# Clustered attention with a feed-forward block on one core: queries laid out lower half first, one copy less, the keys' copies moved to GpSimd and VectorE, and two prices of the planner changed

## The chip, the core and the metric

The kernel runs on one core of a Trainium2 chip. The core has a matrix engine (TensorE, in the profile PE, with its weight loads as PEld), a vector engine (VectorE, DVE), a scalar engine (ScalarE, ACT), a general engine (GpSimd, POOL) and a queue engine that only starts DMA transfers here (SyncE, SP). Each engine carries out its own list of instructions in order; semaphores make one wait for another. The time is device microseconds of the core, from one launch; lower is better.

## The reference

Two parts follow each other. Attention has 4 batches, 8 heads, 768 positions and 64 dimensions per head. Each query and each key is assigned to one of 16 clusters of its head, and a query sees only keys of its own cluster. The output, 3072 tokens of 512 features, goes through a feed-forward block of 2048 hidden units with a clipped square as its activation.

```python
def _attn_ref(q, k, v, centroids):
    ...
    q_assign = np.argmax(np.einsum('bhsd,hcd->bhsc', q_n, c_n), axis=-1)
    k_assign = np.argmax(np.einsum('bhsd,hcd->bhsc', k_n, c_n), axis=-1)
    mask = q_assign[:, :, :, None] == k_assign[:, :, None, :]
    scores = scale * np.matmul(q, k.transpose(0, 1, 3, 2))
    scores = np.where(mask, scores, -1000000000.0)
    scores = scores - np.max(scores, axis=-1, keepdims=True)
    attn = np.exp(scores)
    attn = attn / (np.sum(attn, axis=-1, keepdims=True) + 1e-09)
    return np.matmul(attn, v).astype(np.float32)

def _moe_ref(x, w_in, w_out):
    h = x @ w_in
    g = np.where(h >= 1, h, np.where(h <= -1, 0.0, (h + 1) ** 2 / 4))
    return (g @ w_out).astype(np.float32)
```

(The second function is shortened: its constant beta is 1.) Everything is float32 in and out.

## The kernel before, in words

**Numbers in two halves.** Every float32 operand of a product is scaled by a power of two and split into an upper and a lower float16 half, and a product is formed as upper times lower plus lower times upper plus upper times upper. So most products come in threes.

**Staging.** The work goes by batch (4), by pair of heads (4 per batch, 16 in all, called head pairs) and by chunk of 256 queries (3). For a head pair, `kv_load` loads keys, queries and values, `kv_scale` finds the scales, `kq_split` makes the halves and `assign` finds the clusters. A score group (`at_scores`) is for 128 queries of one head; there are 192. `at_soft` forms the exponentials on ScalarE, splits them, and transposes them by DMA into the tile `pT` (11 of them early on by TensorE, in groups of six float32 transposes). `at_av` multiplies with the values into `banka`, where each product uses 64 columns of the array. `ffn1` and `ffn2` are the feed-forward block for 256 tokens and 256 hidden units. Its weights are loaded and split in the opening only (`w_load`, `w_bits`, `w_sum`, `w_split`; tiles `w` and `wk`).

**Keys and queries of a head pair.** `kn` and `qn` are tiles of 128 partitions x 12 blocks x 2 x 64 in float16 (in the profile `n`, in the first batch also `x`, `o` and `g`): for each of the 12 blocks (2 heads x 6 tiles of positions) two halves of 64. `kq_split` fills the keys as (lower, upper) and the queries as (upper, lower), and a DMA transpose turns each into `kT` and `qT` (in the tile `kvq`), so that one product over 128 rows gives both mixed terms. `assign` multiplies `kT` and `qT` with the centroids and finds the nearest cluster on VectorE. Then it reuses the same tiles: the first half of each block becomes a code of the cluster (16 columns, written by VectorE; the other 48 of the keys are cleared by GpSimd), the second half must hold the upper halves, for the keys times `phi`, a factor of the head pair. For the keys that is a GpSimd product in place (lines 640 to 642). For the queries, whose second half still holds the lower halves, ScalarE makes a second copy of the upper ones from the float32 queries (lines 645 and 646). Two more DMA transposes give `k1` and `q1`, which carry the third term and the mask. `kT` too is multiplied by `phi` in place, by ScalarE (lines 643 and 644), before the score products read it. The rest of `assign` works out `er`, which the score evictions use.

**Order of the work.** Nothing is issued directly. A recorder collects all operations with their dependences, and `Recorder.issue` plans them: up to eight rounds of a list schedule (`forward`), with due times worked out backwards (`backward`), and the best plan's order is issued engine by engine. What an operation is thought to take comes from `Recorder.price` (line 76): it sees engine, operation and sizes. For TensorE the price is by columns, with a separate rule, `half`, for products with at most 64 columns of weights, and before 75 us of planned time TensorE's prices are doubled. So a change of a price or of one operation can move instructions in the whole program. Since everything is issued from one line, all instructions in the profile have line 292; groups are told apart by their tiles.

Of the kernel before, what the change touches and what calls it, by code (L numbers as in the profile page):

```python
# [11 lines left out]
F32 = mybir.dt.float32  # L12
U32 = mybir.dt.uint32
AF = mybir.ActivationFunctionType
ALU = mybir.AluOpType
# [22 lines left out]
class Recorder:  # L38
# [37 lines left out]
    def price(self, eng, op, out, ins, kw):  # L76

        if "dma" in op:
            n = 1
            for k in out.shape:  # L80
                n *= k
            kb = n * mybir.dt.size(out.dtype) / 1024

            return 33, 79.0 if kb == 2 else kb, "transpose" in op
        n = max(self.free(a) for a in [out] + ins[:1])
        ps = any(a.space == PSUM for a in ins)
        cols = sum(isinstance(kw.get(k), bass.AP) for k in ("scale", "bias", "scalar", "scalar1", "scalar2"))
        if eng == "tensor":
            n = self.free(ins[1])
            half = self.free(ins[0]) <= 64 and n > 100  # L90
            if op == "transpose":
                n *= 2
            elif ins[1].dtype == F32:
                n *= 4
            return n / 4.8 + 1.2 if half else max(n / 2.4 + 2.5, 24)
        if eng == "scalar":
            cols += kw.get("accum_out") is not None
            first = n == 1 and kw.get("scale") == 0.0
            return 93 + n / 1.2 + 94 * cols - 43 * ps + 1283 * first
        if eng == "vector":  # L100
            wide = [a for a in ins if self.free(a) > 1 or n == 1]
            wait = 400 if not ps and (len(wide) > 1 or op in ("tensor_scalar", "tensor_copy")) else 0
            fast = 1
            if op in ("tensor_scalar", "tensor_copy") and not ps:
                fast = 4 if mybir.dt.size(out.dtype) == 2 and mybir.dt.size(ins[0].dtype) == 2 and n > 64 else 2
            return 68 + n / 0.96 / fast + 61 * cols + 20 * (op == "reciprocal") + wait
        return 55 + n * (2.03 if op == "tensor_tensor" else 0.9 if op == "memset" else 3.5)
# [243 lines left out]
def tile_clustered_attention_moe(  # L351
# [11 lines left out]
    B, H, S, D = q.shape  # L363
    C = cent.shape[1]
# [4 lines left out]
    P = 128  # L369
# [21 lines left out]
    rec = Recorder(tc)  # L391
# [37 lines left out]
    def early():  # L429

        return rec.step < EARLY

    def misc(*shape):
        return (row_banks if early() else hid)(*shape, dtype=F32)
# [144 lines left out]
    def transpose(out, nat):  # L579
        rec.sync.dma_start_transpose(out=out, in_=nat.rearrange("p n a d -> p (n a d)"))  # L580

    def kq_split(b, hp):

        e = KV[b, hp]
        for x, lower, at in (("k", 0, 0), ("q", 1, 4)):
            nat = e[x + "n"]
            src = e[x].rearrange("p j (t d) -> p (j t) d", d=D)
            col = "kq".index(x)
            split(nat[:, :, 1 - lower], nat[:, :, lower], src, e["sc"][:, col : col + 1])
            e[x + "T"] = view(e["parts"][at], [2 * T, P], F16)  # L590
            transpose(e[x + "T"], nat)
# [6 lines left out]
    def assign(b, hp):  # L598

        e = KV[b, hp]  # L600
        n2 = 2 * T
        n4 = 2 * n2
        z1 = misc(n4, C)
        for i, x in enumerate("kq"):
            with rec.group():
                for n in range(n2):
                    h = 2 * hp + n // T
                    for a in range(2):
                        rec.tensor.matmul(
                            z1[:, i * n2 + n],  # L610
                            e[x + "T"][:, n],
                            cT[:, a, h * C : (h + 1) * C],
                            start=(a == 0),
                            stop=(a == 1),
                        )
# [9 lines left out]
        rec.vector.tensor_reduce(out=mx, in_=z1, op=ALU.max, axis=AX.X)  # L625
        rec.vector.tensor_tensor(out=z1, in0=z1, in1=wide(mx), op=ALU.subtract)

        rec.gpsimd.memset(e["kn"][:, :, 0, C:], 0.0)
        for i, x in enumerate("kq"):
            rec.vector.tensor_scalar(  # L630
                out=e[x + "n"][:, :, 0, :C],
                in0=z1[:, i * n2 : (i + 1) * n2],
                scalar1=0.0,
                scalar2=-ONE if x == "k" else ONE,
                op0=ALU.not_equal if x == "k" else ALU.is_equal,
                op1=ALU.mult,
            )

        kn, qn = e["kn"], e["qn"]
        rec.gpsimd.tensor_tensor(  # L640
            out=kn[:, :, 1], in0=kn[:, :, 1], in1=e["phi"].unsqueeze(2).to_broadcast([P, n2, D]), op=ALU.mult
        )
        kf = e["kT"].rearrange("p n q -> p (n q)")
        rec.scalar.activation(out=kf, in_=kf, func=AF.Copy, scale=e["phi"])
        qf = e["q"].rearrange("p j (t d) -> p (j t) d", d=D)
        rec.scalar.activation(out=qn[:, :, 1], in_=qf, func=AF.Copy, scale=e["sc"][:, 1:2])
        for x, part in (("k", 3), ("q", 2)):
            e[x + "1"] = view(e["parts"][part], [n2, P], F16)
            transpose(e[x + "1"], e[x + "n"])

        pn = misc(2, C)
        with rec.group():
# [457 lines left out]
```

## Time and profile before

| what | value |
|---|---|
| median of 3 runs | 921.69 us (919.97 to 922.86) |
| the profiled execution's own time | 923.2 us |
| its span, first to last instruction | 921.4 us |
| mean granted TensorE clock | 0.981 |
| TensorE busy | 812.9 us, 88% |
| ScalarE busy | 691.6 us, 75% |
| VectorE busy | 604.1 us, 66% |
| GpSimd busy | 565.6 us, 61% |
| share of the DMA engines taken by transfers | 77.0% |

The span in 40 slices of 23 us each, as tenths of a slice:

```profile
PE   0256668988998999999989999998998999999998
DVE  5998777887888565646776665547886555554222
ACT  6989997977778677778868778777887677777232
POOL 1766786975565577765555667655656677666221
DMA  9979956796899958978999778888899768576100
```

A 9 means 90% or more of the slice. TensorE fills up over the first eight slices, while the other engines are full from the second on. The shares of the whole span are averages over parts with different limits, so the prediction reads them by stretch.

### The profile page before, as it was taken

The numbers are of one execution on the slowest core, as the hardware profiler recorded it, in microseconds if no ns is written. First come the engines' busy times: TensorE is split into PE (matmuls) and PEld (weight loads), VectorE is DVE, ScalarE is ACT, GpSimd is POOL, SyncE is SP. The second block draws the span as 40 slices with busy tenths as digits, with TensorE's granted clock in tenths as the row PEclk, the third lists the DMA queues.
The fourth block names the chain that finished last, engine by engine and source line by source line (L and its number), as shares of the span: only waits on it lengthen the run. The fifth ranks groups of instructions, "written<-read, shape, count | busy, mean of one in ns | idle before, by whom it ended". The sixth has DMA issues, their size and how long they took to land.

```text
span 921.4 us, 19471 instructions
## 1 busy us (share of the span) xinstructions
PE 812.9 (88%) x7414; PEld 559.2 (61%) x7414; DVE 604.1 (66%) x1322; ACT 691.6 (75%) x1173; POOL 565.6 (61%) x520
## 2 busy tenths in 40 slices
PE   0256668988998999999989999998998999999998
PEld 0234446655766766676666666766666666666664
DVE  5998777887888565646776665547886555554222
ACT  6989997977778677778868778777887677777232
POOL 1766786975565577765555667655656677666221
PEclk9998789999999999999999999999999999999999
DMA  9979956796899958978999778888899768576100
GB/s 293 251 176 218 238 127 145 155 188 139 200 179 159 189 109 144 181 130 193 196 186 163 147 150 166 149 175 170 184 179 174 136 136 129 108 130 113 19 24 24
DMA packets 409535, 144.39 MB, mean 157 GB/s; under 512 B 386272, under 2 KB 401632, under 8 KB 409440
## 3 DMA queue, kind: packets, MB, share of 16 engines
q1 hardware_dynamic: 409440, 143.14, 77.0%
q8 instruction: 58, 0.95, 0.4%
q14 instruction: 37, 0.30, 0.1%
HBM read 40.40 MB, written 6.29 MB: 51 GB/s over the span
## 4 chain that ended last, share of the span: by engine, by line
PE 65%; DVE 10%; ACT 6%; issue 5%; POOL 3%; ACTq 0%; DVEq 0%; POOLq 0%
PE bank L292 47%; PE banka L292 10%; PE bankh L292 8%; DVE sS L292 3%; DVE r L292 2%; ACT sS L292 2%; DVE bank L292 2%; POOL hl L292 1%; ACT w L292 1%; DVE bankh L292 1%; DVE mx L292 1%; ACT hl L292 1%; POOL g L292 1%; ACT r L292 1%; DVE n L292 0%
## 5 line engine op out<-in xcount | busy, mean ns | idle before, releaser
L292 POOL TENSOR_TENSOR hl<-sS,hl 128x768 f16<-128x768 f32 x181 | 303.9, 1683 | 148.7 <-ACT hl L292 115.9
L292 PE MATMUL bank<-w,g 128*128 128x512 f16 x1152 | 271.1, 379 | 0.3 <-POOL g L292 0.2
L292 PEld LDWEIGHTS <-w 128*128 128x128 f16 x2304 | 224.4, 98 | 66.8 <-issue 23.0
L292 DVE CUSTOM_DVE_ANT_0 sS<-bank,zero,er 128x768 f32<-128x768 f32 x192 | 194.3, 1012 | 97.7 <-PE bank L292 67.8
L292 PEld LDWEIGHTS <-kvq 128*64 128x64 f16 (+1 forms) x3264 | 191.1, 106 | 86.2 <-issue 41.3
L292 ACT ACTIVATE sS<-sS,sbi 128x768 f32<-128x768 f32 x192 | 179.2, 933 | 83.9 <-DVE sbi L292 80.2
L292 POOL TENSOR_TENSOR g<-r,g 128x512 f16<-128x512 f32 x96 | 112.6, 1173 | 122.8 <-ACT g L292 119.2
L292 PEld LDWEIGHTS <-g 128*128 128x128 f16 x1152 | 110.7, 98 | 119.1 <-issue 2.1
L292 PE MATMUL bank<-kvq 128*128 128x384 f16 x768 | 162.4, 336 | 19.3 <-DVE sbi L292 14.1
L292 ACT CAST hl<-sS 128x768 f16<-128x768 f32 x181 | 148.3, 825 | 4.9 <-DMA pT<-hl 3.7
L292 PE MATMUL bank<-x,w 128*128 128x256 f16 x1032 | 123.9, 272 | 10.5 <-DVE r L292 5.2
L292 ACT ACTIVATE r<-r,f_ra,f_rs 128x512 f32<-128x512 f32 x96 | 77.8, 810 | 70.7 <-DVE r L292 69.7
L292 PE MATMUL banka<-pT,kvq 128*64 128x256 f16 x1728 | 106.4, 279 | 0.0
L292 DVE TENSOR_SCALAR r<-bank,f_lo,f_hi 128x512 f32<-128x512 f32 x64 | 51.6, 807 | 51.0 <-PE bank L292 41.9
L292 POOL TENSOR_TENSOR w<-w 128x1024 f32<-128x1024 f32 (+1 forms) x28 | 59.8, 2143 | 33.9 <-ACT w L292 32.0
L292 ACT CAST g<-r 128x512 f16<-128x512 f32 x96 | 58.8, 612 | 25.2 <-DVE r L292 18.7
L292 DVE SCALAR_TENSOR_TENSOR r<-bank,f_gs,r 128x512 f32<-128x512 f32 x64 | 47.9, 749 | 24.3 <-ACT r L292 15.6
L292 PE MATMUL bank<-wk,w 128*128 128x256 f16 x504 | 61.1, 272 | 3.1 <-DVE bank L292 2.1
L292 PE MATMUL bankh<-x,w 128*128 128x256 f16 x504 | 60.1, 273 | 2.2 <-DVE r L292 2.0
L292 PEld LDWEIGHTS <-ones 128*128 128x128 bf16 x244 | 17.2, 107 | 53.5 <-issue 38.5
L292 DVE TENSOR_SCALAR r<-bankh,f_lo,f_hi 128x512 f32<-128x512 f32 x32 | 25.8, 806 | 25.4 <-PE bankh L292 19.8
L292 ACT ACTIVATE n<-kvq,sc 128x768 f16<-128x768 f32 x42 | 37.1, 924 | 1.7 <-DVE sc L292 1.6
(158 smaller groups left out, 842.5 us busy)
## 6 DMA issues: line engine op xcount, KB each, us to landing
w<-in_moe_w_in_dram SPq DMA_DIRECT2D x14, 512.0 KB, 4.8
w<-in_moe_w_out_dram SPq DMA_DIRECT2D x14, 512.0 KB, 4.7
kvq<-in_k_dram SPq DMA_DIRECT2D x16, 384.0 KB, 3.6
kvq<-in_q_dram SPq DMA_DIRECT2D x16, 384.0 KB, 3.8
kvq<-in_v_dram SPq DMA_DIRECT2D x16, 384.0 KB, 4.1
out_dram<-o SPq DMA_DIRECT2D x11, 512.0 KB, 3.0
o<-in_v_dram SPq DMA_DIRECT2D x8, 384.0 KB, 3.7
pT<-hl SPq DMA_TRANSPOSE x181, 4.0
```

Of the source, the lines that this page charges most:

```text
L292: fn(*args, **kw)
```

## The change

Three things are done.

1. The order of the halves is turned around: keys (upper, lower), queries (lower, upper). The product over 128 rows gives the same two mixed terms. For the queries, the second half now holds the upper halves from the start, and ScalarE's second copy of them is left out, once per head pair.
2. For the keys the second half now holds the lower halves, so GpSimd's product with `phi` reads the first half and writes the second. It is recorded at the beginning of `assign`, ahead of the clearing and of the cluster code, which overwrite the first half. The scaling of `kT` by `phi` goes from ScalarE (`activation`) to VectorE (`tensor_scalar`), recorded behind the two transposes.
3. In `Recorder.price` a transpose is no longer counted twice, but as any float32 operand is, four times (its second operand is the float32 identity), and the fixed part of the `half` products goes from 1.2 to 9 ns.

```diff
-            if op == "transpose":
-                n *= 2
-            elif ins[1].dtype == F32:
+            if ins[1].dtype == F32:
                 n *= 4
-            return n / 4.8 + 1.2 if half else max(n / 2.4 + 2.5, 24)
+
+            return n / 4.8 + 9 if half else max(n / 2.4 + 2.5, 24)
...
-        for x, lower, at in (("k", 0, 0), ("q", 1, 4)):
+        for x, lower, at in (("k", 1, 0), ("q", 0, 4)):
...
         z1 = misc(n4, C)
+
+        kn = e["kn"]
+        rec.gpsimd.tensor_tensor(
+            out=kn[:, :, 1], in0=kn[:, :, 0], in1=e["phi"].unsqueeze(2).to_broadcast([P, n2, D]), op=ALU.mult
+        )
...
-        kn, qn = e["kn"], e["qn"]
-        rec.gpsimd.tensor_tensor(
-            out=kn[:, :, 1], in0=kn[:, :, 1], in1=e["phi"].unsqueeze(2).to_broadcast([P, n2, D]), op=ALU.mult
-        )
-        kf = e["kT"].rearrange("p n q -> p (n q)")
-        rec.scalar.activation(out=kf, in_=kf, func=AF.Copy, scale=e["phi"])
-        qf = e["q"].rearrange("p j (t d) -> p (j t) d", d=D)
-        rec.scalar.activation(out=qn[:, :, 1], in_=qf, func=AF.Copy, scale=e["sc"][:, 1:2])
         for x, part in (("k", 3), ("q", 2)):
             e[x + "1"] = view(e["parts"][part], [n2, P], F16)
             transpose(e[x + "1"], e[x + "n"])
+        kf = e["kT"].rearrange("p n q -> p (n q)")
+        rec.vector.tensor_scalar(out=kf, in0=kf, scalar1=e["phi"], scalar2=None, op0=ALU.mult)
```

The whole plan comes out in another order; three places matter below. The first is ScalarE's list in the opening, from the weights' passes to the scaling of the second head pair's keys. `n_73` and `x_70` with `sc` are float16 halves of queries, `kvq` with `phi` is `kT` being scaled, `kvq` with `sv` the values' halves, `w` and `wk` the weights. Before:

```order
L292 CAST w_76<-w_76 128x1024
L292 ACTIVATE n_73<-kvq_61,sc_137 128x12x64
L292 ACTIVATE kvq_61<-kvq_61,phi_141 128x1536
L292 ACTIVATE kvq_62<-kvq_62,sv_146 128x768
L292 ACTIVATE w_76<-w_76 128x1024
L292 ACTIVATE x_70<-kvq_63,sc_137 128x12x64
L292 ACTIVATE x_69<-kvq_63,sc_137 128x12x64
L292 ACTIVATE wk_66<-w_76 128x1024
L292 ACTIVATE w_76<-w_76,w_sw_158 128x1024
L292 CAST w_76<-w_76 128x1024
L292 ACTIVATE kvq_62<-kvq_62,phi_142 128x1536
```

Now, down to the first exponential (`sS_83`):

```order
L291 ACTIVATE x_69<-kvq_63,sc_137 128x12x64
L291 ACTIVATE x_70<-kvq_63,sc_137 128x12x64
L291 ACTIVATE wk_66<-w_76 128x1024
L291 ACTIVATE g_71<-kvq_64,sc_138 128x12x64
L291 ACTIVATE w_76<-w_76,w_sw_157 128x1024
L291 CAST w_76<-w_76 128x1024
L291 ACTIVATE w_76<-w_76 128x1024
L291 ACTIVATE o_65<-kvq_64,sc_138 128x12x64
L291 ACTIVATE kvq_63<-kvq_63,sv_146 128x768
L291 ACTIVATE kvq_64<-kvq_64,sv_146 128x768
L291 ACTIVATE sS_83,rs_163<-sS_83,sbi_159 128x768
```

The third copy per head pair (`n_73` alone) and both scalings with `phi` are gone, and the splits of the third and fourth head pair have moved up ahead of the first exponential.

The second place is VectorE's list at the first head pair, from the cluster codes (`n_72`, `n_73`) on. Before:

```order
L292 TENSOR_SCALAR n_73<-bank_79 128x12x16
L292 SCALAR_TENSOR_TENSOR kvq_61<-kvq_61,sv_146 128x768
L292 TENSOR_SCALAR wk_66<-wk_66 128x1024
L292 TENSOR_SCALAR has_150<-bankh 128x32
L292 RECIPROCAL bank_79<-es_140 128x1
L292 TENSOR_SCALAR bank_79<-bank_79 128x2
L292 SCALAR_TENSOR_TENSOR w_76<-w_76,wk_66 128x1024
L292 TENSOR_TENSOR bank_79<-bank_79,has_150 128x192
L292 TENSOR_REDUCE bank_78<-bank_78 128x1
```

Now:

```order
L291 TENSOR_SCALAR n_73<-bank_79 128x12x16
L291 RECIPROCAL sc_137<-bank_79 128x2
L291 TENSOR_SCALAR bank_79<-bank_79 128x1
L291 TENSOR_SCALAR wk_66<-wk_66 128x1024
L291 TENSOR_SCALAR has_150<-bankh 128x32
L291 SCALAR_TENSOR_TENSOR w_76<-w_76,wk_66 128x1024
L291 TENSOR_TENSOR bank_79<-bank_79,has_150 128x192
L291 TENSOR_REDUCE bank_78<-bank_78 128x1
L291 TENSOR_SCALAR kvq_61<-kvq_61,phi_141 128x1536
```

The scaling of `kT` has come in as the last row, between a weights' pass and the rest of the assignment.

The third place is GpSimd's list at its beginning, with the product `n_72` with `phi`, the clearing (`MEMSET`) and the weights' products (`w_76`). Before:

```order
L292 TENSOR_SCALAR idu<-idf 128x128
L292 TENSOR_TENSOR w_76<-w_76 128x1024 x2
L292 MEMSET n_72 128x12x48
L292 TENSOR_TENSOR w_76<-w_76 128x1024 x2
L292 COPY w_all_215<-w_am_0_114 128x2
L292 TENSOR_TENSOR w_76<-w_76 128x1024
L292 COPY w_all_213<-w_iw_0_122 128x2
L292 TENSOR_TENSOR n_72<-n_72,phi_141 128x12x64
```

Now:

```order
L291 TENSOR_SCALAR idu<-idf 128x128
L291 TENSOR_TENSOR n_72<-n_72,phi_141 128x12x64
L291 MEMSET n_72 128x12x48
L291 TENSOR_TENSOR w_76<-w_76 128x1024 x3
L291 TENSOR_TENSOR n_74<-n_74,phi_142 128x12x64
```

The product of the first head pair has moved from behind five of the weights' products to ahead of all of them. On TensorE, 23 score groups instead of 22 stand ahead of the first feed-forward product, and the list behind the last value product is as it was.

More of the change, by code (lines that the diff above doesn't have):

```diff
@@ L626, in assign @@
         rec.vector.tensor_tensor(out=z1, in0=z1, in1=wide(mx), op=ALU.subtract)
-        rec.gpsimd.memset(e["kn"][:, :, 0, C:], 0.0)
+        rec.gpsimd.memset(kn[:, :, 0, C:], 0.0)
         for i, x in enumerate("kq"):
```

## The prediction

> **What bounds the kernel now.** I read the page's engine totals first, then busy time by stretch, then groups of instructions and the chain of waits. The times are of one profiled execution: 923.2 us in all, a span of 921.4 and 1.8 around it. It lies 1.5 above the median of the runs, 921.69, so the sum is made against 923.2 and 1.5 is taken off at the end.
>
> ```profile
> span 921.4 us, 19471 instructions
> PE 812.9 (88%) x7414; PEld 559.2 (61%) x7414; DVE 604.1 (66%) x1322; ACT 691.6 (75%) x1173; POOL 565.6 (61%) x520
> ```
>
> TensorE (PE) is busy for 88% and its work doesn't change, so a gain can only come out of the 108.5 us in which it stands idle. The busy times of each engine by stretch say where those are (the columns: stretch, its length, busy time of PE, weight loads, DVE, ACT and POOL, granted clock, DMA share, GB/s).
>
> ```profile
> 0.00:20.00 20.00, 1.18 (x9) 1.06 (x10) 9.68 (x27) 12.00 (x19) 3.84 (x26) 1.00 0.91 285
> 20.00:60.00 40.00, 13.50 (x167) 10.34 (x167) 38.41 (x82) 33.90 (x39) 26.85 (x16) 1.00 0.94 244
> 60.00:140.00 80.00, 50.88 (x474) 34.71 (x473) 65.08 (x162) 75.59 (x113) 57.27 (x46) 0.81 0.81 186
> 140.00:200.00 60.00, 52.69 (x478) 36.76 (x477) 49.10 (x127) 53.07 (x100) 48.33 (x43) 1.00 0.79 161
> 200.00:240.00 40.00, 36.84 (x352) 25.80 (x351) 32.78 (x84) 28.44 (x50) 24.29 (x23) 1.00 0.81 176
> 240.00:320.00 80.00, 76.29 (x766) 53.00 (x764) 62.16 (x129) 62.15 (x104) 45.49 (x42) 1.00 0.91 171
> 320.00:440.00 120.00, 119.02 (x1057) 81.38 (x1055) 72.96 (x149) 92.10 (x168) 81.06 (x72) 1.00 0.81 153
> 440.00:520.00 80.00, 74.32 (x739) 51.54 (x738) 57.25 (x127) 61.95 (x107) 46.60 (x44) 0.98 0.94 176
> 520.00:600.00 80.00, 79.96 (x691) 54.36 (x690) 47.68 (x99) 61.17 (x113) 55.93 (x50) 1.00 0.79 153
> 600.00:720.00 120.00, 113.30 (x1088) 77.84 (x1085) 82.31 (x178) 94.19 (x161) 71.19 (x64) 1.00 0.91 179
> 720.00:880.00 160.00, 160.00 (x1389) 110.61 (x1387) 76.22 (x151) 105.78 (x191) 96.68 (x91) 1.00 0.59 106
> ```
>
> In the first 200 us PE is idle for 200 - (1.18 + 13.50 + 50.88 + 52.69) = 81.8. From 200 to 720 it is idle for 3.2 + 3.7 + 1.0 + 5.7 + 0.0 + 6.7 = 20.3, of which 16.1 lie in the three stretches (240 to 320, 440 to 520, 600 to 720) in which the keys and queries of the next batch are prepared. From 720 to 880 it never stops. In the opening the bound changes hands: from 20 to 60 VectorE (DVE) is busy 38.4 of 40 us, from 60 to 140 ScalarE (ACT) 75.6 of 80. A look at the exponentials alone, from 56.5 to 173, says the same (after the bar: busy, mean ns; after the second bar: idle time just before them and what ended it).
>
> ```profile
> L292 ACT ACTIVATE sS<-sS,sbi 128x768 f32<-128x768 f32 x31 | 29.0, 934 | 8.7 <-DVE sbi L292 8.4
> ```
>
> Thirty-one exponentials pass there in 116.5 us, and ACT stood waiting before them for only 8.7: what stands ahead of each in ACT's order sets the pace, more than its input.
>
> **What is taken from ScalarE.** Per head pair it loses one copy of the queries' upper halves and the scaling of the transposed keys; there are 16 pairs. The rows give min/median/max in ns.
>
> ```profile
> L292 ACT ACTIVATE n<-kvq,sc x42: 918/921/937, 10.8 to 705.0; 128x768 f16<-128x768 f32 x42
> L292 ACT ACTIVATE kvq<-kvq,phi x16: 1559/1572/1585, 37.7 to 696.2; 128x1536 f16<-128x1536 f16 x16
> ```
>
> One of every three of the first row goes (two stay, the splits of keys and queries): 16 x 0.921 = 14.7, and 16 x 1.572 = 25.2, together 39.9 us of 691.6. Those of the first batch stand in the opening:
>
> ```profile
> 36.84 0.93 ACT L292 ACTIVATE n<-kvq,sc 128x768 f16<-128x768 f32 x1
> 37.68 1.56 ACT L292 ACTIVATE kvq<-kvq,phi 128x1536 f16<-128x1536 f16 x1
> 46.91 1.57 ACT L292 ACTIVATE kvq<-kvq,phi 128x1536 f16<-128x1536 f16 x1
> 61.25 0.92 ACT L292 ACTIVATE n<-kvq,sc 128x768 f16<-128x768 f32 x1
> 78.94 0.94 ACT L292 ACTIVATE x<-kvq,sc 128x768 f16<-128x768 f32 x1
> 80.70 1.57 ACT L292 ACTIVATE kvq<-kvq,phi 128x1536 f16<-128x1536 f16 x1
> 91.01 1.58 ACT L292 ACTIVATE kvq<-kvq,phi 128x1536 f16<-128x1536 f16 x1
> 96.76 0.96 ACT L292 ACTIVATE o<-kvq,sc 128x768 f16<-128x768 f32 x1
> ```
>
> That is 4.06 us before 60, where DVE binds, and 5.97 from 60 to 140, where ACT binds. The 5.97 I count in full. Of the 4.06 I count half, 2.0: the freed time lets ACT do passes over the weights earlier, but DVE feeds it there. Opening, ACT's part: -8.0, between -6 and -10.
>
> **What VectorE gets.** Sixteen scalings of 128x1536 in 16 bits, SBUF to SBUF. The trace has no such form. The nearest is a pass with one input over 32-bit words, in two sizes, 512 and 1024:
>
> ```profile
> L292 DVE TENSOR_SCALAR wk<-wk x18: 414/696/1910, 13.8 to 199.3; 128x1024 uint32<-128x1024 uint32 x14, 128x512 uint32<-128x512 uint32 x4
> L292 DVE SCALAR_TENSOR_TENSOR n<-kvq,sc,n x28: 1002/1013/2457, 11.7 to 689.1; 128x768 f16<-128x768 f32 x28
> L292 DVE SCALAR_TENSOR_TENSOR n<-kvq,sc,n 128x768 f16<-128x768 f32 x28 | 36.6, 1323 | 1.6 <-ACT n L292 1.6
> ```
>
> From 414 to 696 are 0.28 for 512 words, so about 0.13 is fixed; 1536 elements at the same rate per element take 0.13 + 3 x 0.28 = 0.97, at the same rate per byte 0.55. The second row shows the other end: the same operation takes 1.00 or 2.46. The long ones coincide with GpSimd:
>
> ```profile
> 41.93 2.66 POOL L292 TENSOR_TENSOR w<-w 128x1024 f32<-128x1024 f32 x1
> 42.90 2.50 DVE L292 SCALAR_TENSOR_TENSOR x<-kvq,sc,x 128x768 f16<-128x768 f32 x1
> ```
>
> The VectorE operation, 1.0 us alone, ends with or just after the GpSimd one. On average over 28 this adds 1.323 - 1.013 = 0.31. I take 0.97 + 0.31 = 1.28 for one scaling, between 0.55 and 2.46; all sixteen, 20.5 us. In the opening two of the four fall into the stretch in which DVE is 96% busy: +2.5 (1.1 to 4.9). The other two are covered: DVE would have 65.1 + 2.6 = 67.7 of the remaining 74 us from 60 to 140. If that cover were gone they would cost 2.6.
>
> The Trainium skill, "SBUF - State Buffer", section "Who interferes with whom", speaks against this move: a VectorE operation in a two-port mode and a GpSimd operation exclude each other for a whole instruction, whichever begins first. ScalarE's version was free of that. By that rule the new operation can hold up GpSimd as well as be held up; the row of 2.50 agrees with the second half, and no row here shows the first for an operation of this form. In "VectorE: DVE Perf Modes", "The perf-mode tier table", a 16-bit scaling of 2048 elements is put at 693 ns; by that the sixteen would be nearer 0.55 each, an estimate, and the sum for VectorE 16 x 0.86 = 13.8 us with the same average wait.
>
> **What GpSimd and the queues get.** GpSimd's product does what it did, in the same form, so its price stays; only its input is the other half, and it now needs nothing but the first transpose and stands ahead of the clearing of that half. I count 0. The bound below is the delay it can give the weights' products behind it in the first order, one such product, -1.5 to +1.5.
>
> ```profile
> L292 POOL TENSOR_TENSOR n<-n,phi x14: 1463/1468/1911, 34.4 to 703.0; 128x768 f16<-128x768 f16 x14
> ```
>
> The transposes on SP's queue are as many and as large; the second one of the queries waits for one writer less.
>
> **The planner's two prices** carry no work of their own; they move the order. A product group of the values (36 halves of 256 columns and 8 of 128) was planned as 36 x 54.5 + 8 x 27.9 = 2.19 us and is now 36 x 62.3 + 8 x 35.7 = 2.53. A group of six fp32 transposes was planned as 6 x 0.109 = 0.66, now 1.30.
>
> ```profile
> 144.53 2.31 PE banka L292 x44
> 57.74 1.51 PE L292 MATMUL bank<-idf,sS 128*128 128x128 f32 x6 [2.20 <-POOL w L292]
> ```
>
> The first price leaves 2.31 on the other side, 0.12 short before and 0.22 long now; the second comes nearer. Neither tells the sign. The first feed-forward product stands behind 23 groups of scores where it stood behind 22, and everything behind the last value product stands as before, so I take 0 with 4 us either way.
>
> **The batch changes** (200 to 720). ACT loses 12 x (0.921 + 1.572) = 29.9 us there, DVE gains 12 x 1.28 = 15.4. PE's loss is 20.3 in all, which is the ceiling. The chain from 425 to 520 says who is late in it:
>
> ```profile
> by line: PE bank L292 31.1%; issue 16.5%; PE bankh L292 9.1%; PE banka L292 7.3%; DVE sS L292 4.7%; DVE r L292 4.2%; POOL hl L292 3.7%; POOL g L292 3.7%; ACT n L292 3.3%; ACT sS L292 2.9%; DVE bank L292 2.1%; ACT g L292 1.9%; ACT r L292 1.7
> ```
>
> ACT's lines are 9.8% of 95 us, 9.3 us; DVE's 11.0%, 10.4. ACT's work falls by 10 of 62 (16%) at a change, so about 1.5 us goes; DVE's rises by 5.1 of 57 (9%), so 0.9 comes back. Three changes: -4.5 + 2.7 = -1.8, between -8 and +9. What is late next is the DMA queue, 0.94 busy there, which the change leaves alone.
>
> **Sum**: opening -8.0 + 2.5 = -5.5, order 0, GpSimd 0, batch changes -1.8: -7.3 on 923.2 gives 915.9, and 914.4 on the scale of the median. I say **914**, by itself 909 to 919.
>
> **Rivals.** *The opening is held by something else.* For it: DMA is 0.91 to 0.94 busy up to 60, DVE 96%. Against it: 60 to 140, where DMA is at 0.81 and DVE at 81%. Then ACT's freed time turns into waits, of its -8.0 only the 2.5 that DVE adds are made good, and the batch changes give half of their -1.8: 923.2 - 0.9 - 1.5 = 920.8, with 2 either way.
>
> *The scalings lock against GpSimd* (slower). On VectorE they stand right behind the assignment products and ahead of the reduction that begins the assignment of clusters; everything of that chain and the next score evictions queue behind them. If each takes 2.46, the opening has +4.9 against -6, and at the batch changes 12 x 2.46 = 29.5 us are added to DVE. Of what is late there beside PE and the unexplained part, DVE has 11.0 of 28.2 (ACT 9.8, GpSimd 7.4), so 0.39 x 29.5 = +11.5 reach the path, less 4.5 from ACT: together +5.9, or 927.6. It decides from the point at which more than half of the sixteen last over 2 us. For it: GpSimd is 57 to 72% busy in all the stretches in which these run. Against it: the median of the 28 is 1.013, so most escape.
>
> *ACT holds all of it.* The opening gives the full 10, and the batch changes -6, with DVE's share absorbed: 16 less, 906. For it: 8.7 us of waiting in 116; against it DVE's 38.4 of 40.
>
> **Numbers.** Forecast 0.48, ACT holds all 0.20, held by something else 0.18, lock 0.14. Faster by over 0.3% (2.8 us, about what a measurement of this kernel can tell from no change) means below 918.9: 0.48 x 0.95 + 0.20 + 0.18 x 0.2 = 0.69. Within it: 0.15. Slower: 0.16. The range 904 to 924 holds the first three cases and leaves out most of the lock case.
>
> **What would show it.** Right: ACT busy near 652, DVE near 625; the 31 exponentials done some 5 us sooner than by 173; PE idle before 200 down by about 5; the new DVE rows with a median near 1.0. Wrong: the new rows with a median over 2; PE's idle time from 200 to 720 above 25; or the opening unchanged with DVE at 95% on to 140. A longer PE-bound stretch in spite of an earlier opening would say that the new order costs more than the work saved.

## The result, and the profile after

| kernel | median | ratio to before, 95% interval |
|---|---|---|
| before, in the same comparison | 921.62 us | 1 |
| changed | 928.57 us (927.32 to 930.03) | 1.0081 (1.0064 to 1.0098) |

The change makes the kernel slower by 7 us, where 7 us less were forecast. The engine totals of the changed kernel, from its page:

```profile
span 927.7 us, 19424 instructions
PE 819.9 (88%) x7414; PEld 563.6 (61%) x7414; DVE 612.3 (66%) x1338; ACT 657.6 (71%) x1141; POOL 572.4 (62%) x520
```

The work moved as it should. ScalarE (ACT) lost 691.6 - 657.6 = 34.0 us (39.9 by the sum of the durations, which overlap their neighbours a little: the copy of 0.93 us that began at 36.84 reached past the scaling's begin at 37.68), VectorE (DVE) gained 8.2 (20.5 were counted), GpSimd (POOL) 6.8. TensorE (PE) has the same 7414 products, and is busy 7.0 us longer over them (819.9 for 812.9). Its idle time, 927.7 - 819.9 = 107.8 us, is what it was (108.5). So in these two executions the longer span is not TensorE waiting, but TensorE taking longer over the same products. The stretches say where (columns as in the prediction):

```profile
20.00:60.00 40.00, 12.60 (x135) 8.74 (x135) 37.82 (x81) 31.77 (x40) 25.12 (x14) 0.97 0.88 243
60.00:140.00 80.00, 51.72 (x450) 35.61 (x447) 68.35 (x159) 64.70 (x99) 58.90 (x47) 0.67 0.82 186
140.00:200.00 60.00, 51.86 (x443) 36.37 (x443) 44.82 (x106) 50.17 (x91) 47.34 (x37) 0.89 0.63 137
240.00:320.00 80.00, 74.72 (x761) 50.85 (x758) 64.82 (x134) 53.69 (x96) 47.91 (x43) 1.00 0.95 169
440.00:520.00 80.00, 75.65 (x777) 52.63 (x774) 62.77 (x133) 55.45 (x99) 48.18 (x45) 0.98 0.93 173
600.00:720.00 120.00, 114.28 (x1123) 79.67 (x1121) 83.01 (x182) 88.72 (x157) 74.61 (x67) 1.00 0.93 176
```

From 60 to 140 ScalarE is busy 64.7 us where it was 75.6. What the forecast took for the bound is eased, and yet nothing comes of it. TensorE is as busy as before from 60 to 200 (103.6 us both times), but with 893 matmuls where there were 952, at a granted clock of 0.67 and 0.89 where it was 0.81 and 1.00. TensorE's idle time from 200 to 720 is 20.0 us, before 20.3; from 200 on the two kernels differ little.

How far the attention is at a given time can be counted by the exponentials, ScalarE's pass over each score group. All 192 take about (851 - 57) / 191 = 4.2 us each on the way through the kernel before. The groups of instructions up to 110 us and from 110 to 200, first before, then changed:

```profile
L292 ACT ACTIVATE sS<-sS,sbi 128x768 f32<-128x768 f32 x12 | 11.3, 939 | 5.5 <-DVE sbi L292 5.5
L292 ACT ACTIVATE sS<-sS,sbi 128x768 f32<-128x768 f32 x27 | 25.1, 930 | 3.7 <-DVE sbi L292 3.3
```

```profile
L291 ACT ACTIVATE sS<-sS,sbi 128x768 f32<-128x768 f32 x14 | 13.1, 935 | 6.7 <-DVE sbi L291 6.7
L291 ACT ACTIVATE sS<-sS,sbi 128x768 f32<-128x768 f32 x23 | 21.5, 936 | 6.5 <-DVE sbi L291 6.4
```

At 110 the changed kernel is two exponentials ahead; in the next 90 us it does 23 against 27. (The one that runs across 110 us stands in both of its groups.) By 200 us it has begun 36 where 39 had begun. The 31st starts at 177.3 us where it started at 172.3, the 37th at 201.6 where it was 190.9, the last at 857.1 where it was 850.9. So the loss is made between 110 and 200 us, and some of it is won back later. In the chain of waits of the changed kernel TensorE's own work is slow there (start and duration in us):

```profile
129.04 4.06 PE banka L291 x42
145.84 4.21 PE banka L291 x40
```

This is the product of the weights with the values; the like of it took 2.31 us for 44 in the row before.

### The profile page after: what moved, and what is told of

The parts are those of the page before. It is cut to its first block, busy times and chain, and to the rows that moved or that the text cites. A ratio compares the mean times of both kernels' runs of the same rounds, so it can differ in the third digit from the quotient of the medians.

```text
span 927.7 us, 19424 instructions
## 1 busy us (share of the span) xinstructions
PE 819.9 (88%) x7414; PEld 563.6 (61%) x7414; DVE 612.3 (66%) x1338; ACT 657.6 (71%) x1141; POOL 572.4 (62%) x520
## 4 chain that ended last, share of the span: by engine, by line
PE 66%; DVE 10%; issue 6%; POOL 4%; DMA 2%; ACT 2%; ACTq 0%; DVEq 0%; POOLq 0%; SPq 0%
PE bank L291 48%; PE banka L291 10%; PE bankh L291 8%; DVE r L291 2%; DVE sS L291 2%; POOL hl L291 2%; DMA pT<-hl 2%; DVE bank L291 1%; DVE wk L291 1%; POOL g L291 1%; ACT sS L291 1%; DMA kvq<-n 1%; POOL w L291 0%; DVE n L291 0%; ACT hl L291 0%
## 5 line engine op out<-in xcount | busy, mean ns | idle before, releaser
L291 PEld LDWEIGHTS <-w 128*128 128x128 f16 x2304 | 224.5, 98 | 63.2 <-issue 20.5
L291 POOL TENSOR_TENSOR g<-r,g 128x512 f16<-128x512 f32 x96 | 114.7, 1195 | 130.9 <-ACT g L291 129.1
L291 PE MATMUL bank<-kvq 128*128 128x384 f16 x768 | 165.1, 341 | 23.5 <-DVE sbi L291 11.6
L291 PE MATMUL banka<-pT,kvq 128*64 128x256 f16 x1728 | 108.4, 282 | 0.1
L291 ACT ACTIVATION_READ_ACCUMULATOR sS<-sS,sbi 128x1 f32 x192 | 35.9, 187 | 0.0
```

What stands on the lines that cost most here:

```text
L291: fn(*args, **kw)
```

## The experiments

Three things could have cost it: the work that was moved, the order that the planner made of it, or TensorE's clock. They are told in the order in which they were run. The table has them all; "exponentials" are those up to 110 us and from 110 to 200 us, "clock" is the granted clock from 100 to 150 us, both of the profiled execution.

| kernel | median | ratio, 95% interval | exponentials | clock |
|---|---|---|---|---|
| before | 920.2 to 922.3 | 1 | 12 + 27 | 0.85 |
| changed | 928.57 | 1.0081 (1.0064 to 1.0098) | 14 + 23 | 0.66 |
| changed work, prices of before | 938.33 | 1.0183 (1.0154 to 1.0212) | 13 + 25 | 0.69 |
| work of before, both new prices | 927.83 | 1.0076 (1.0050 to 1.0103) | 14 + 25 | 0.90 |
| changed, 64-column price of before | 933.68 | 1.0148 (1.0123 to 1.0173) | 13 + 23 | 0.73 |
| changed, transposes' price of before | 939.37 | 1.0206 (1.0179 to 1.0232) | 12 + 23 | 0.75 |
| order of before, no second copy | 921.16 | 0.9994 (0.9976 to 1.0012) | 12 + 28 | 0.86 |
| order of before, no copy, scalings on VectorE | 927.08 | 1.0057 (1.0037 to 1.0077) | 12 + 27 | 0.83 |
| changed order, work of before | 945.41 | 1.0255 (1.0234 to 1.0275) | 12 + 24 | 0.74 |
| before, 64-column price 1.3 | 925.80 | 1.0045 (1.0030 to 1.0060) | 13 + 24 | 0.69 |
| before, 64-column price 1.1 | 932.70 | 1.0138 (1.0113 to 1.0163) | 12 + 24 | 0.78 |
| order of before, neither copy nor scalings | 921.35 | 1.0010 (0.9995 to 1.0025) | 12 + 27 | 0.86 |
| changed, scalings back on ScalarE | 928.75 | 1.0092 (1.0063 to 1.0121) | 12 + 24 | 0.80 |
| changed, TensorE kept at work | 923.88 | 1.0035 (1.0022 to 1.0048) | 12 + 25 | 0.83 |
| changed, twice that work | 926.66 | 1.0046 (1.0028 to 1.0064) | 12 + 25 | 0.83 |
| before, TensorE kept at work | 922.62 | 1.0012 (0.9995 to 1.0029) | 13 + 27 | 0.93 |
| price 1.1, TensorE kept at work | 933.10 | 1.0125 (1.0098 to 1.0152) | 12 + 23 | 0.77 |

**Work and prices apart.** The four ways to put half of the change in; each is planned anew. The work alone has the change's edits in `kq_split` and `assign` and leaves `price` as it was:

> The turned halves, the left-out copy and the moved scalings, with the planner's prices of before. Theory A (the new prices' order loses the time, above all through TensorE's lower granted clock between 60 and 200 us): faster than before, 912 to 919 us, granted clock from 60 to 200 back near 0.9. Theory B (the scalings on VectorE and their lock with GpSimd lose it): slower than before, 925 to 931, as the whole change is.

The prices alone, on the kernel before:

```diff
-            if op == "transpose":
-                n *= 2
-            elif ins[1].dtype == F32:
+            if ins[1].dtype == F32:
                 n *= 4
-            return n / 4.8 + 1.2 if half else max(n / 2.4 + 2.5, 24)
+            return n / 4.8 + 9 if half else max(n / 2.4 + 2.5, 24)
```

> The kernel before with the two new prices alone. Theory A: slower, 926 to 932, since the order alone does it. Theory B: 919 to 924, no change.

The change with one of the two prices put back, first the 64-column products, then the transposes:

```diff
-            return n / 4.8 + 9 if half else max(n / 2.4 + 2.5, 24)
+            return n / 4.8 + 1.2 if half else max(n / 2.4 + 2.5, 24)
```

> The whole change but for the price of the products with 64 columns, which stays 1.2. Theory A, with the 64-column price to blame (it overstates a group by 0.22 us): 914 to 921. Theory A, with the transposes to blame: 926 to 931. Theory B: 925 to 931.

```diff
-            if ins[1].dtype == F32:
+            if op == "transpose":
+                n *= 2
+            elif ins[1].dtype == F32:
                 n *= 4
```

> The whole change but for the price of the fp32 transposes, which stays doubled, not fourfold. Theory A, with the 64-column price to blame: 926 to 931. Theory A, with the transposes to blame: 914 to 921. Theory B: 925 to 931.

Measured: +1.83%, +0.76%, +1.48% and +2.06%. All but the second lie beyond the ranges of both theories. Each half by itself costs, the work most, and both together (+0.81%) cost less than the work with any other pair of prices. Parts that don't add up point to the order, since each of these kernels has a plan of its own; that is an argument, not yet a test. So the order had to be held still.

**The order held still.** An operation can be planned as one thing and issued as another; then every engine's list stays as planned. (The traces of these runs show each engine's list unchanged but for the operations named.) With the order of before, first only the second copy of the queries is dropped, so that the third product works on the lower halves:

```diff
-        rec.scalar.activation(out=qn[:, :, 1], in_=qf, func=AF.Copy, scale=e["sc"][:, 1:2])
+        rec.add("scalar", "activation", lambda *x, **y: None, (),
+            dict(out=qn[:, :, 1], in_=qf, func=AF.Copy, scale=e["sc"][:, 1:2]))
```

> The kernel before, planned with all its work and issued in exactly its order, but the 16 second copies of the queries' upper halves are not issued on ScalarE (the third product so works on the lower halves and the output is off; nothing else is left out). Theory P (a plan's order decides, the work saved is a gain): 914 to 920 us. Theory W (the work as it is moved makes it slower, through VectorE): 919 to 923, since VectorE has nothing more to do here.

Then also the scaling of the keys is issued on VectorE, in the place of the program at which ScalarE had it:

```diff
-        rec.scalar.activation(out=kf, in_=kf, func=AF.Copy, scale=e["phi"])
+        rec.add("scalar", "activation",
+            lambda *x, **y: nc.vector.tensor_scalar(out=kf, in0=kf, scalar1=e["phi"], scalar2=None, op0=ALU.mult), (),
+            dict(out=kf, in_=kf, func=AF.Copy, scale=e["phi"]))
```

> As the one before, and the 16 scalings of the transposed keys are issued on VectorE at the place in the global order where ScalarE had them. So the order is that of before and the work that of the change (the copies left out, output off in the same way). Theory P: 908 to 921. Theory W: 925 to 935.

The other way about, the order of the changed kernel with the work of before:

> The changed kernel in exactly its order, with the old work: the scalings are issued on ScalarE where VectorE had them, and ScalarE makes a second copy of the queries' upper halves just ahead of the queries' second transpose (the values are the same). Theory P: no faster than the change, 927 to 940. Theory W: faster than the change, 915 to 924.

And the kernel before with a price that says nothing of any work, to see what a new plan costs by itself:

```diff
-            return n / 4.8 + 1.2 if half else max(n / 2.4 + 2.5, 24)
+            return n / 4.8 + 1.3 if half else max(n / 2.4 + 2.5, 24)
```

> The kernel before with one price nudged without meaning: 1.3 instead of 1.2 ns for the fixed part of the products with 64 columns. Theory P: another plan, and slower than before like the others, 923 to 935. Theory W, and any theory in which the particular prices matter: 919 to 923.

Dropping 14.7 us of ScalarE's work moved nothing: 0.9994. Giving VectorE the scalings, at the same order, cost 5.9 us more (1.0057). These two went as the theory of the work expected (W). The nudge of 0.1 ns cost 4.1 us (1.0045), with a loss from 110 to 200 us like that of the change (24 exponentials), and in the changed order the old work takes 945.4: these two went against it, and 945.4 lies beyond what the theory of the order (P) expected.

The four corners of order and work do not add up. The new work costs 0.57% in the old order, and in the new order it saves 945.4 - 928.6 = 16.8 us. The new order costs 2.55% with the old work, and with the new work 1.0081 against 1.0057, which the intervals do not tell apart. So neither the order nor the work alone can be given the loss. What a piece of work is worth depends on the order it stands in; in the new order the old work also stands at places that no plan chose for it, so part of the 16.8 us can be that.

**All of ScalarE's relief, and two more plans.** With the order of before, the scaling too is issued on no engine:

```diff
-            lambda *x, **y: nc.vector.tensor_scalar(out=kf, in0=kf, scalar1=e["phi"], scalar2=None, op0=ALU.mult), (),
+            lambda *x, **y: None, (),
```

> The kernel before, with its order of instructions on every engine kept; the second copy of the queries' upper halves and the scaling of the transposed keys are issued on no engine, so the keys stay unscaled here: the full relief of ScalarE (39.9 us) with nothing given to VectorE. Theory (at this order ScalarE's relief is worth nothing, and the loss of the run with the scalings on VectorE is VectorE's own added work): 919 to 922, ratio 0.997 to 1.001, which leaves about 6 us to VectorE's scalings. Rival (the relief gains, and the scalings on VectorE cost twice what the earlier pair of runs showed): 914 or less, ratio under 0.993. My prediction's step for ScalarE alone, -8.0 in the opening and -4.5 at the batch changes, would make it 909.

Its totals, and its exponentials up to 110 us and from 110 to 200:

```profile
span 922.1 us, 19425 instructions
PE 813.8 (88%) x7414; PEld 560.5 (61%) x7414; DVE 607.7 (66%) x1322; ACT 656.3 (71%) x1141; POOL 567.0 (61%) x520
```

```profile
L292 ACT ACTIVATE sS<-sS,sbi 128x768 f32<-128x768 f32 x12 | 11.2, 934 | 8.0 <-DVE sbi L292 8.0
L292 ACT ACTIVATE sS<-sS,sbi 128x768 f32<-128x768 f32 x27 | 25.2, 933 | 4.5 <-DVE sbi L292 4.3
```

ScalarE does 35.3 us less than before (656.3 for 691.6), and the exponentials come at the same times: 12 and 27 as before. Part of what ScalarE saved stands as waiting before them: 8.0 us up to 110 where it was 5.5, and in the whole program 94.5 where it was 83.9 (first before, then this kernel):

```profile
L292 ACT ACTIVATE sS<-sS,sbi 128x768 f32<-128x768 f32 x192 | 179.2, 933 | 83.9 <-DVE sbi L292 80.2 <-POOL hl L292 1.9 <-DVE bank L292 0.2
```

```profile
L292 ACT ACTIVATE sS<-sS,sbi 128x768 f32<-128x768 f32 x192 | 179.2, 933 | 94.5 <-DVE sbi L292 90.7 <-POOL hl L292 1.9 <-POOL n L292 0.2
```

At this order ScalarE's list is not what paces the opening. The time is 1.0010 (0.9995 to 1.0025), and the 4.3 us up to the run with the scalings on VectorE (1.0057; by the intervals 2 to 7 us) belong to VectorE's added work. They show no loss in the opening. The stretches from 240, 440 and 600 us, first with neither, then with the scalings on VectorE:

```profile
240.00:320.00 80.00, 76.55 (x771) 53.57 (x769) 62.25 (x130) 54.45 (x96) 46.92 (x43) 1.00 0.95 175
440.00:520.00 80.00, 72.97 (x735) 50.34 (x734) 59.87 (x130) 55.54 (x100) 48.21 (x44) 1.00 0.93 177
600.00:720.00 120.00, 113.90 (x1111) 78.61 (x1108) 83.00 (x180) 85.60 (x153) 71.79 (x65) 1.00 0.91 179
```

```profile
240.00:320.00 80.00, 74.58 (x755) 52.04 (x754) 63.71 (x129) 54.08 (x96) 46.18 (x42) 1.00 0.93 170
440.00:520.00 80.00, 71.85 (x718) 49.23 (x717) 60.00 (x128) 53.78 (x98) 46.98 (x43) 0.98 0.91 173
600.00:720.00 120.00, 112.67 (x1101) 77.58 (x1099) 86.44 (x182) 83.66 (x150) 73.18 (x64) 1.00 0.89 175
```

TensorE stands idle 2.0 + 1.1 + 1.2 = 4.3 us longer in them. That this equals the 4.3 us above is chance: these are single executions, 2.7 us apart, and the stretch before the first of them goes the other way by 1.8 us, again first with neither:

```profile
200.00:240.00 40.00, 36.62 (x348) 25.47 (x346) 32.93 (x85) 27.88 (x52) 23.98 (x24) 1.00 0.78 161
200.00:240.00 40.00, 38.44 (x364) 26.93 (x362) 33.04 (x88) 27.66 (x50) 25.80 (x24) 1.00 0.88 179
```

Over the whole span TensorE is idle for 924.7 - 813.1 = 111.6 us with the scalings and 922.1 - 813.8 = 108.3 without. The 96th of the 192 exponentials starts at 458.4 with them and at 460.1 without, the last at 854.2 and 851.5. So in these executions the loss lies behind 458 us.

Two more plans: the changed kernel with the scalings back on ScalarE, and the kernel before with the price nudged the other way.

```diff
-        rec.vector.tensor_scalar(out=kf, in0=kf, scalar1=e["phi"], scalar2=None, op0=ALU.mult)
+        rec.scalar.activation(out=kf, in_=kf, func=AF.Copy, scale=e["phi"])
```

> The changed kernel with the scaling of the transposed keys on ScalarE as before (planned anew): one part undone. Theory (what costs the 10 us in the opening is the new plan, whatever the work): still slower than before, 923 to 935, with the loss between 120 and 200 us. Rival (the scalings on VectorE make the loss): 918 to 922, and the opening as in the kernel before.

```diff
-            return n / 4.8 + 1.2 if half else max(n / 2.4 + 2.5, 24)
+            return n / 4.8 + 1.1 if half else max(n / 2.4 + 2.5, 24)
```

> The kernel before with the fixed part of the price of a 64-column product 1.1 ns instead of 1.2: a price change that says nothing of any work, and moves a comparable number of TensorE's rows as 1.3 did. Theory (the order before is a lucky draw among plans of the same quality): 924 to 930, the loss again between 120 and 200 us. Rival (plans near the old prices are all as good, and 1.3 was one bad draw): 919 to 923.

Undoing the move of the scalings gives nothing back (1.0092). 1.1 in place of 1.2 costs more than the whole change: 1.0138. Its two groups of exponentials:

```profile
L292 ACT ACTIVATE sS<-sS,sbi 128x768 f32<-128x768 f32 x12 | 11.2, 933 | 4.7 <-DVE sbi L292 4.7
L292 ACT ACTIVATE sS<-sS,sbi 128x768 f32<-128x768 f32 x24 | 22.4, 932 | 5.6 <-DVE sbi L292 5.6
```

Again 24 where 27 were, with the work of before to the last instruction. Every one of the eight plans other than that of before does 23 to 25 exponentials between 110 and 200 us; the five kernels in the order of before, whatever their work, do 27 or 28. But this count is not the whole loss, and the loss is not of one kind. The work of before with both new prices (1.0076) starts its 96th exponential at 458.0 us, where before it was 457.9, and its last at 857.8, where it was 850.9: it loses its time later. Its totals, and those of the plan of price 1.3:

```profile
PE 812.7 (88%) x7414; PEld 560.7 (60%) x7414; DVE 614.7 (66%) x1322; ACT 692.0 (75%) x1173; POOL 564.8 (61%) x520
PE 819.8 (89%) x7414; PEld 563.5 (61%) x7414; DVE 613.5 (66%) x1322; ACT 690.7 (75%) x1173; POOL 571.6 (62%) x520
```

Their spans are 928.4 and 924.5 us. In the first TensorE is busy as before (812.9), and the loss is idle time (115.7 for 108.5); in the second the idle time is 104.7, and the loss is busy time, as in the changed kernel.

**The clock.** The low granted clock could be what these plans lose by, or only follow from their waits. In the changed kernel, its order kept, TensorE repeats four products of 384 columns ahead of each of the eleven groups of fp32 transposes of the opening, into the bank that the transposes overwrite (`row` and `keys` are the score group's own queries and keys; their two lines are left out here):

```diff
...
-                    rec.tensor.transpose(to, sf[:, i * P : (i + 1) * P], idf)
+                    def turn(*x, i=i, to=to, **y):
+                        for h in range(2 if i == 0 else 0):
+                            for _ in range(2):
+                                nc.tensor.matmul(pS[:, h, :HS], row, keys[:, h * HS : (h + 1) * HS], start=True, stop=True)
+                        nc.tensor.transpose(to, sf[:, i * P : (i + 1) * P], idf)
...
+                    rec.add("tensor", "transpose", turn, (to, sf[:, i * P : (i + 1) * P], idf), {})
```

> The changed kernel with its order kept; ahead of each of the eleven groups of six fp32 transposes of the opening, TensorE repeats four products of 384 columns into the bank that the transposes then overwrite: it has work in the time in which it waits for ScalarE's exponential (0.64 us at full clock, 1.3 at half). Theory (the low granted clock between 100 and 150 us costs the 10 us): the granted clock there rises from 0.66 to 0.85 or more, the exponentials of the first passes come sooner, and the time falls by 5 to 9: 919 to 924. Rival (the clock only follows the waits that the order makes, and is no cause): the clock may rise or not, the time stays within 3 us of the changed kernel's 928.6 or grows by part of the 7 to 14 us of added products: 927 to 935.

The time fell to 1.0035 (1.0022 to 1.0048), 4.2 us below the changed kernel by the ratios; forty-four useless products made the kernel faster. The stretch from 100 to 150 us, first of the changed kernel, then of this one:

```profile
100.00:150.00 50.00, 33.12 (x241) 22.89 (x241) 35.49 (x92) 41.06 (x62) 34.03 (x29) 0.66 0.67 177
```

```profile
100.00:150.00 50.00, 36.30 (x311) 25.01 (x308) 40.06 (x103) 43.47 (x69) 37.51 (x30) 0.83 0.74 188
```

Between 100 and 150 the clock went from 0.66 to 0.83. Three kernels were to tell whether that is what parts the two: the kernel before with the same products, the changed one with twice as many, and the plan of price 1.1 with them.

```diff
-                            for _ in range(2):
+                            for _ in range(4):
```

> The kernel before with its order kept and the same forty-four repeated products ahead of the eleven groups of fp32 transposes of the opening. In the changed kernel they took off about 5 us. Theory (the low clock of the changed kernel's opening, 0.66 between 100 and 150 us, is a cause of its loss that the kernel before has less of, 0.85): here they gain less, 0 to 2 us, ratio 0.997 to 1.001. Rival (any plan gains the same 5 us from them, so the clock doesn't part the two kernels): ratio 0.993 to 0.996.

> The changed kernel with its order kept and eight repeated products in each of the eleven places instead of four (1.3 us at full clock, 2.6 at half). Theory (the clock's share of the loss is larger than the 5 us that four products brought back): granted clock between 100 and 150 above 0.9, time 919 to 923. Rival (what is left, some 3 us, is the order itself, and the added products now delay the transposes): 924 to 930.

> The plan that the price of 1.1 ns gives (932.7 us) with its order kept and the same forty-four repeated products. Theory (the low clock is a common part of the losses of all these plans): 4 to 8 us faster, 925 to 929. Rival (this plan's granted clock between 100 and 150, 0.78, is not what holds it): 931 to 935.

The kernel before gained nothing (1.0012, 0.9995 to 1.0029), though its clock rose there from 0.85 to 0.93. Twice the products in the changed kernel gave 1.0046, no more than once. The plan of price 1.1 gained about 1 us, within its interval (1.0125 for 1.0138); its clock stayed where it was (0.77 for 0.78). And among executions of one kernel the mean clock doesn't foretell the time: in 62 of the kernel before it goes from 0.975 to 0.991, with no slope (the correlation with the time is -0.02). So the clock is not the common cause of the losses: with both new prices TensorE is busy no longer than before, and the time is lost all the same. In the changed kernel some 4 of the 7 us came back together with a higher clock. That makes the clock a likely part of its loss; the added products also shift what follows them, and no run separates the two. The rest is left to order and work together. Which feature of the order of before carries the stretch from 110 to 200 was not found: every part of it is tied to the others by the plan, and no run moved one part of the order alone.

No kernel beat the one before.

## Why the prediction was wrong

**The opening, ScalarE's part: -8.0.** This is the step that failed. It took ScalarE's 75.6 of 80 busy us, and the 8.7 us of waiting before 31 exponentials, to mean that what stands ahead of each in ScalarE's list sets the pace. With all of the work taken away and the order kept, the time didn't move (1.0010), and the waiting grew instead. A list that is 94% busy may still be waiting for the same inputs, with its other work filling the gaps. What set the pace in its place is open; the trace names only what the exponentials wait for, an operand that VectorE writes (`sbi`). The rival "held by something else" had the right mechanism for ScalarE (freed time turns into waits). Its 920.8 did not come even with the order kept: with all of the change's work that gave 927.1, because of VectorE's part.

**TensorE: its work doesn't change.** From this the prediction took that time could only be won or lost in the 108.5 us in which TensorE stands idle. The products stayed the same, but their time did not: 819.9 us for 812.9, at a granted clock of 0.67 and 0.89 from 60 to 200 us, while the idle time stayed (107.8). No term of the sum stood for this.

**The order: 0 with 4 either way.** The second failure, of sign and of size. It was argued from the prices' distance to the measured groups and from two places of the list that were nearly unchanged. (The group of transposes chosen for it, 1.51 us, is one of the slow ones: the group at 85.1 us took 0.87 at a granted clock of 1.00, the one at 67.0 us 1.54 at 0.50. At full clock the old price, 0.66, is the nearer.) Measured without any change of work, three other plans lie at 1.0045, 1.0076 and 1.0138: 4 to 13 us, none below before. The prediction's last sentence on what would show it wrong comes near the case: TensorE's busy time did grow, but the opening was earlier only up to 110 us.

**VectorE: +2.5 in the opening.** In the changed kernel over-sized in duration, and by the run in the order of before in the wrong place. Its row, minimum, median and maximum in ns:

```profile
L291 DVE TENSOR_SCALAR kvq<-kvq,phi x16: 605/612/2389, 37.4 to 708.6; 128x1536 f16<-128x1536 f16 x16
L291 DVE TENSOR_SCALAR kvq<-kvq,phi 128x1536 f16<-128x1536 f16 x16 | 12.6, 786 | 2.1 <-PE bank L291 2.1
```

Alone it takes 0.61 us where 0.97 was taken, and 0.79 on average where 1.28 was, 12.6 us for all where 20.5 were. The estimate by bytes (0.55) was the nearer end, as the estimate from the Trainium skill's "VectorE: DVE Perf Modes", "The perf-mode tier table", had it. But the duration goes with the order. In the order of before, where they stand in ScalarE's old places, the same scalings came out as predicted, 0.98 in the median and 1.19 on average:

```profile
L646 DVE TENSOR_SCALAR kvq<-kvq,phi x16: 583/984/2496, 36.0 to 700.2; 128x1536 f16<-128x1536 f16 x16
L646 DVE TENSOR_SCALAR kvq<-kvq,phi 128x1536 f16<-128x1536 f16 x16 | 19.0, 1188 | 0.4 <-PE bankh L292 0.4
```

There they cost nothing that shows in the opening (12 and 27 exponentials) and some 4 us behind it.

**Batch changes: -1.8.** At the order of before ScalarE's relief gave nothing there (16.6 us of idle time in the three stretches, before 16.1), not -4.5, and VectorE's load 4.3 more in them, not +2.7, against the 1.8 less just ahead of them. The changed kernel itself stands where it stood: TensorE is idle there for 5.3 + 4.4 + 5.7 = 15.4 us, before 16.1.

**GpSimd: 0.** Its first product, moved to the front, waits 14.8 us, and all the weights' products stand behind it. The first of those began at 21.4 us where it began at 16.1, and by 55 us eight had begun where nine had. That is more than the 1.5 us of the bound; VectorE was part of it (the last 1.5 us of the wait were for VectorE's `w`), and no run took this apart. The lock is seen from GpSimd's side too. The two copies among `x` and `g` took 1.48 and 1.46 us before, and now:

```profile
L291 POOL TENSOR_TENSOR n<-n,phi 128x768 f16<-128x768 f16 x14 | 22.7, 1619 | 19.7 <-DVE bank L291 14.8 <-DVE phi L291 2.6 <-DVE er L291 2.3
L291 POOL TENSOR_TENSOR g<-g,phi 128x768 f16<-128x768 f16 x1 | 2.2, 2235 | 1.8 <-DVE w_sw L291 1.8
L291 POOL TENSOR_TENSOR x<-x,phi 128x768 f16<-128x768 f16 x1 | 2.2, 2232 | 1.5 <-DVE w_sw L291 1.5
```

The Trainium skill's "SBUF - State Buffer", "Who interferes with whom", says that either engine can be held for a whole instruction. From VectorE's and GpSimd's timelines, the pair of the longest scaling and the pair of the product of `x`:

```profile
80.25 2.13 POOL L291 TENSOR_TENSOR w<-w 128x1024 f16<-128x1024 f32 x1 [1.64 <-ACT w L291]
63.51 2.23 POOL L291 TENSOR_TENSOR x<-x,phi 128x768 f16<-128x768 f16 x1 [1.50 <-DVE w_sw L291]
```

```profile
80.42 2.39 DVE L291 TENSOR_SCALAR kvq<-kvq,phi 128x1536 f16<-128x1536 f16 x1
63.42 0.99 DVE L291 SCALAR_TENSOR_TENSOR o<-kvq,sc,o 128x768 f16<-128x768 f32 x1
```

The scaling began behind GpSimd's product and ended 0.43 us after it; the product of `x` began 0.09 behind a VectorE operation of 0.99, and took 0.77 more than 1.46. So these rows agree with both halves of the rule. But only one of the sixteen scalings lasted over 2 us, and three in the order of before, so the rival "lock" (from half of them on) is refuted as a cause. That its 927.6 lies near the time measured is chance.

**ACT holds all of it** (906) fell with the first step. Of the signs named ahead, ScalarE near 652 (657.6) and TensorE's idle time from 200 to 720 (20.0, before 20.3) held and told nothing; VectorE stayed at 612.3 where 625 was named. The exponentials' was the one that decided: the 31st came 5 us later where 5 us sooner was named.

## What to carry to other kernels

A busy engine that waits little is not shown to be the bound: the test is to take its work away with the order of everything else held still, and here 35 us of it were worth nothing. Where a planner sets the order, compare a change with the plans that meaningless nudges of a price give, or pin the order. This kernel sat at the good end of the four plans measured for the same work (0 to 1.4%), and any edit draws again. Work handed to another engine is to be priced at the stages in which that engine is late, and not only where it was taken from. And an engine's busy time is no constant: the same products took TensorE 805 to 826 us in the runs here.

## What the hardware showed unexpectedly

In the changed kernel's opening TensorE's granted clock is 0.66 from 100 to 150 us, while TensorE is busy for two thirds of that time (33.1 of 50 us). In the kernel with the repeated products the same four take (start and duration in us, from its timeline):

```profile
94.68 0.81 PE L780 MATMUL bank<-kvq 128*128 128x384 f16 x4 [2.26 <-DVE sbi L291]
111.41 1.44 PE L780 MATMUL bank<-kvq 128*128 128x384 f16 x4 [1.23 <-DVE sbi L291]
```

The granted clock was 1.00 at the first and 0.50 at the second. The Trainium skill's "TensorE: Matmul & The Clock Gate", "HAM oscillation — how this bites in real kernels", has the loss as half of the time spent at half clock. By that it would be, as an estimate, about 51.72 x 0.33 + 51.86 x 0.11 = 23 us for the changed kernel from 60 to 200, and 9.7 for the one before. The repeated products gave part of it back. All that were added took 12.7 us in the changed kernel and 10.3 in the one before, from their rows and the totals of both (first the changed kernel's):

```profile
L780 PE MATMUL bank<-kvq 128*128 128x384 f16 x44 | 12.7, 429 | 8.0 <-DVE sbi L291 8.0
L783 PE MATMUL bank<-kvq 128*128 128x384 f16 x44 | 10.3, 361 | 4.8 <-DVE sbi L292 4.8
```

```profile
PE 821.3 (89%) x7458; PEld 564.9 (61%) x7458; DVE 615.8 (67%) x1338; ACT 657.6 (71%) x1141; POOL 570.8 (62%) x520
PE 815.4 (89%) x7458; PEld 559.7 (61%) x7458; DVE 603.4 (66%) x1322; ACT 690.9 (75%) x1173; POOL 565.4 (62%) x520
```

So TensorE's own products took 821.3 - 12.7 = 808.6 us where they took 819.9, and 815.4 - 10.3 = 805.1 where they took 812.9. These 11.3 and 7.8 us of TensorE's time brought the time down by 4 us in the one and by nothing in the other. Where other engines are late too, time that TensorE saves turns into waiting, and here most of what the slow clock took from TensorE was not lost by the kernel.
